# Keys turned once for two units: a turned block of the first batch kept in device memory

## The chip, the cores and the metric

The kernel runs on one core of a Trainium2 chip. Its engines are TensorE (PE, with its weight loads PEld), VectorE (DVE), ScalarE (ACT), GpSimd (POOL) and SyncE (SP), which here issues all the DMAs. Each engine works through its own instructions in the order of the program; semaphores hold an instruction until what it needs is there. The metric is the device time of one execution in microseconds. Before the change it is 1012.05 us, the median of three runs (1011.5 to 1013.39).

## The reference

Three layers one after another: a causal attention with decay, and two feed-forward layers, all in float32.

```python
scores = (1/sqrt(D)) * q @ k.T                      # B=4, H=8, S=576, D=64
cum    = cumsum(log(clip(f, 1e-4, 1)))
scores = where(causal, -1e9, scores + cum_i - cum_j)
x      = softmax(scores) @ v                        # to [2304, 512]
h      = x @ moe_w_in                               # d_ff = 2048
x      = (max(h, 0) + alpha * min(h, 0)) @ moe_w_out
h      = x @ moe2_w_in
g      = where(h >= 1, h, where(h <= -1, 0, (h + 1)**2 / 4))
out    = g @ moe2_w_out
```

The weights come as 64-bit floats; the kernel takes their words apart and builds 32-bit values from them.

## The kernel before

The 576 tokens of a batch are cut into two units: the first has the queries 0 to 255 (QA = 256), the second 256 to 575. A unit is worked in four pairs of heads. For a pair the kernel loads K, Q and V, turns K and Q on PE (a matmul against a unit matrix, 128 tokens at a time, into a PSUM bank), copies them back to SBUF, forms scores, exponentials and the product with V, and writes its part of the first layer's input x. Causality means that a first unit needs the keys 0 to 255, a second one all 576.

The first batch (units 0 and 1) goes through `plain_pair` (line 553), the other three through the code from line 822 on. In `plain_pair`, `load_k` (line 563) and `load_q` (567) load the tokens by `load_tok` (467, two DMAs of whole 128-token blocks and one for a remainder of 64), `ktr` (579) turns K in groups of up to KC = 512 tokens, `kcopy` (585) copies each group to the tile `kT`, and `qk` (646) forms the scores of 64 queries, all of which need every `kcopy` of the pair. `kT` has two buffers, taken in turn by the pairs. A pair of the first unit has one group of 256 tokens: two transposes, one copy. A pair of the second unit has two groups, of 512 and 128 tokens (padded): four transposes and one, a copy of 512 columns and one of 128. The keys 0 to 255 are thus loaded and turned twice, once in each unit. In the later batches the kernel already keeps them: `stash` (line 901) writes the turned block to device memory, `reload` (867) reads it back.

Beside the first batch run the conversion of the first layer's weights (`convert`, 1212: load on line 1227, `mag` 1239, `clamp` 1242, `low_exp` 1248, `top` 1256, `bottom` 1261, `hi` 1269, `lo` 1275) and, as soon as the first 256 tokens of x are there, the first layer's slices (`l1_slice`, 1312; matmuls on lines 1323 and 1362).

The order of each engine's instructions is made by a planner, `Order.emit` (line 114). Every piece of work is a task with an engine, an estimated duration, a position (`pos`), what it depends on and which buffers it takes. The planner plays the program through with these estimates: of the engines it takes the one that can start first, and on it, of the tasks that are ready, the one with the lowest position. DMAs are modelled as one line of transfers (`move`, 182). A task on the made-up engines "X" and "Y" costs no engine's time; "Y" lies 1000 ns ahead of SP. So a task that is added or gone changes the estimated ends of what follows, and with them the orders.

Of the kernel before, what the change touches and what calls it, by code (L numbers as in the profile page):

```python
# [9 lines left out]
F32 = mybir.dt.float32  # L10
# [6 lines left out]
P = 128  # L17
# [176 lines left out]
def kernel(  # L194
# [13 lines left out]
    nc = tc.nc  # L208
# [7 lines left out]
    NKB = -(-S // P)  # L216
    SP = NKB * P
# [4 lines left out]
    QA = 256  # L222
# [3 lines left out]
    RATE = 31  # L226
    SMALL = 0.28
    GLEAD = 4
    JO = 0.5
    QOFF = 0  # L230
    WOFF2 = -5
# [47 lines left out]
    def act(n, bias=False):  # L279
        return 93 + n * 0.833 + (93 if bias else 0)  # L280

    def moved(rows, size):
        return rows * (7.5 + size / 24) / 16

    def tok_issue(t0, t1):
        return (980 if t1 - t0 >= P else 0) + (700 if (t1 - t0) % P else 0)
# [8 lines left out]
    def add(eng, dur, fn, pos, *a, **k):  # L295
        return order.add(eng, dur, fn, pos + PRI.get(fn.__name__, 0), *a, **k)
# [7 lines left out]
    ap1 = la.enter_context(tc.tile_pool(name="ap1", bufs=1))  # L304
# [16 lines left out]
    def x2_at(t0, n):  # L321
# [4 lines left out]
    kept, keep_st = {}, {}  # L326
# [16 lines left out]
        out=count, data0=ident, data1=ident, initial=0.0, op0=ALU.add, op1=ALU.bypass)  # L343
# [47 lines left out]
    KC = 4 * P  # L391
# [42 lines left out]
    for j in range(2):  # L434
        nc.gpsimd.affine_select(
            out=PP[j * D:(j + 1) * D, :D], in_=PP[j * D:(j + 1) * D, :D], pattern=[[-1, D]], compare_op=ALU.is_ge,
# [30 lines left out]
    def load_tok(dst, src, b, pr, t0, t1):  # L467
        n = (t1 - t0) // P
        for j in range(2):
            if n:  # L470
                nc.sync.dma_start(
                    out=dst[:, 0:n, j, :],
                    in_=src[b, 2 * pr + j, t0:t0 + n * P, :].rearrange("(c p) d -> p c d", p=P))
        r = t1 - t0 - n * P
        if r:
            nc.sync.dma_start(
                out=dst[:r, n, :, :],
                in_=src[b, 2 * pr:2 * pr + 2, t0 + n * P:t1, :].rearrange("h p d -> p h d"))
# [16 lines left out]
    def f_tr():  # L495
        fb["p"] = ps_a.tile([P, 512], F32, tag=f"s{fP.slot}", name="pst")
        for b_ in range(NKB):
# [6 lines left out]
        out=fb["f"], in0=fb["f"], scalar1=1e-4, scalar2=1.0, op0=ALU.max, op1=ALU.min), -99, [ft], use=[fB])  # L504
    ft = add("ACT", act(S) + 1300, lambda: nc.scalar.activation(out=fb["f"], in_=fb["f"], func=AF.Ln), -99, [ft],
             use=[fB])
# [21 lines left out]
    last = {}  # L528
# [24 lines left out]
    def plain_pair(u, pr, pos_of, prev_pv):  # L553
        b, q0, q1 = units[u]
        n = q1 - q0
        nk = min(S, -(-q1 // P) * P)
        nt, i0 = n // D, q0 // D
        p0 = pos_of(2 * pr)
        v0 = 0 if u else 2 * (pr % 2)
        kb, qb = Buf(R["raw"]), Buf(R["qr1" if pr % 2 else "qr"])  # L560
        kt, qd, st, sw = Buf(R["k"]), Buf(R[f"qd{pr % 2}"]), Buf(R["st"]), Buf(R["sw"])

        def load_k():
            kb.t = RAW[kb.slot]
            load_tok(kb.t, k, b, pr, 0, nk)

        def load_q():
            qb.t = ph["qr"] if pr % 2 else QR[0]
            load_tok(qb.t, q, b, pr, q0, q1)

        lk = last["lk"] = add("SP", tok_issue(0, nk), load_k, p0 - 3, [last.get("lk")], new=[kb], move=moved(2 * nk, 256))
        lq = last["lq"] = add("SP", tok_issue(q0, q1), load_q, p0 - 3, [last.get("lq")], new=[qb], move=moved(2 * n, 256))
        kready = []
        nkp = -(-nk // P) * P
        for t0 in range(0, nkp, KC):
            t1 = min(nkp, t0 + KC)
            pb = Buf(R["s"])

            def ktr(pb=pb, t0=t0, t1=t1):
                pb.t = ps_a.tile([P, 512], F32, tag=f"s{pb.slot}", name="pst")  # L580
                for c in range(t0 // P, t1 // P):
                    nc.tensor.transpose(pb.t[:, c * P - t0:(c + 1) * P - t0],
                                        kb.t[:, c, :, :].rearrange("p j d -> p (j d)"), ident)

            def kcopy(pb=pb, t0=t0, t1=t1):
                if t0 == 0:
                    kt.t = ap1.tile([P, NKB * P], F32, tag=f"k{kt.slot}", name="kT")
                nc.scalar.copy(out=kt.t[:, t0:t1], in_=pb.t[:, :t1 - t0])

            a = last["ktr"] = add("PE", 112 * (t1 - t0) // P, ktr, p0 - 1, [lk, last.get("ktr")], new=[pb], use=[kb])  # L590
            a = add("ACT", act(t1 - t0), kcopy, p0 - 1, [a] + kready, new=[kt] if t0 == 0 else [],
                    use=[pb] if t0 == 0 else [pb, kt])
            kready.append(a)
        pb = Buf(R["s"])
        np_ = -(-n // P)

# [5 lines left out]
        a = last["qtr"] = add("PE", 112 * np_, qtr, p0 - 1, [lq, last.get("qtr")], new=[pb], use=[qb])  # L602
        qready = []
        for j in range(2):
            def qcopy(pb=pb, j=j):
# [6 lines left out]
                              use=[pb, qd] if j else [pb]))  # L612
# [4 lines left out]
        def choose():  # L617
# [6 lines left out]
                 move=moved(2 * nk, 256))  # L624
# [9 lines left out]
        for g in range(-(-nt // 2)):  # L634
# [3 lines left out]
            for t in tiles:  # L638
# [4 lines left out]
                for x, (a0, a1) in enumerate(parts):  # L643
                    sb = Buf(R["s"])

                    def qk(sb=sb, t=t, a0=a0, a1=a1, x=x, n_=len(parts)):
# [6 lines left out]
                        if x == n_ - 1:  # L653
# [3 lines left out]
                    a = last["pqk"] = add("PE", pe4(a1 - a0) + (a1 - a0) / 2.4 + 120, qk, pg,  # L657
                                          kready + qready + crow_ready + [chosen, last.get("pqk")], new=[sb], use=[kt, qd, sw])
# [3 lines left out]
                for x, (sb, a) in enumerate(sbs):  # L662
                    def low(sb=sb, t=t, x=x, w=parts[x][1] - parts[x][0]):
# [4 lines left out]
                                    use=[sb] if st_new else [sb, st]))  # L668
# [133 lines left out]
    for u, pr in head_list():  # L802
        b, q0, q1 = units[u]
# [56 lines left out]
        for j in range(2):  # L860
            def own(j=j, k_of=k_of):
                k_of(j)
# [3 lines left out]
            if again:  # L866
                def reload(j=j, k_of=k_of, kd=kept[b, pr]):
                    nc.sync.dma_start(out=k_of(j).bitcast(F32)[:, :QA], in_=kd[j])
# [28 lines left out]
        if not again and nk == QA:  # L897
            kept[b, pr] = tc.dram_tile([2, P, QA], F32, name=f"kept{b}_{pr}")
            keep_st[b, pr] = []
            for j in range(2):  # L900
                def stash(j=j, k_of=k_of, kd=kept[b, pr]):
                    nc.sync.dma_start(out=kd[j], in_=k_of(j).bitcast(F32)[:, :QA])
# [1119 lines left out]
```

## Time and profile before

| | |
|---|---|
| median of three runs | 1012.05 us |
| profiled execution, its own time | 1014.81 us |
| span of its profile | 1012.9 us |
| PE busy (matmuls) | 995.4 us, 98% |
| PEld busy (weight loads) | 912.3 us, 90% |
| DVE busy | 775.8 us, 77% |
| ACT busy | 651.0 us, 64% |
| POOL busy | 108.7 us, 11% |
| granted clock of PE | 1.00 throughout |
| read and written in device memory | 95.37 MB, 31.51 MB |

Times in the profile are counted from the start of the span. Busy times are sums over the span; matmuls are pipelined and their ends are modelled, so PE shown as busy is not PE at its peak. The first batch and the first layer's conversion take roughly the first 125 us, the other batches' attention with the rest of the first layer go on to about 540 us, and the second layer follows.

### The profile page before, as it was taken

The numbers are of one execution on the slowest core, as the hardware profiler recorded it, in microseconds if no ns is written. First come the engines' busy times: TensorE is split into PE (matmuls) and PEld (weight loads), VectorE is DVE, ScalarE is ACT, GpSimd is POOL, SyncE is SP. The second block draws the span as 40 slices with busy tenths as digits, with TensorE's granted clock in tenths as the row PEclk, the third lists the DMA queues.
The fourth block names the chain that finished last, engine by engine and source line by source line (L and its number), as shares of the span: only waits on it lengthen the run. The fifth ranks groups of instructions, "written<-read, shape, count | busy, mean of one in ns | idle before, by whom it ended". The sixth has DMA issues, their size and how long they took to land.

```text
span 1012.9 us, 19923 instructions
## 1 busy us (share of the span) xinstructions
PE 995.4 (98%) x6736; PEld 912.3 (90%) x6736; DVE 775.8 (77%) x1874; ACT 651.0 (64%) x1675; POOL 108.7 (11%) x222
## 2 busy tenths in 40 slices
PE   7999999999999999999999999999999999999998
PEld 6788899999999999999998888988889998889886
DVE  7999987887778877788738999987868557565552
ACT  6988789888989888988736555544544334332322
POOL 2000033222322222221100000000000000000000
PEclk9999999999999999999999999999999999999999
DMA  8764223231332213421016668486737544454311
GB/s 263 196 216 140 70 79 96 56 75 34 82 100 58 65 48 72 101 54 39 28 32 217 187 181 256 134 290 236 264 115 249 149 127 121 114 177 125 108 49 63
DMA packets 151222, 128.26 MB, mean 127 GB/s; under 512 B 82720, under 2 KB 121648, under 8 KB 151120
## 3 DMA queue, kind: packets, MB, share of 16 engines
q1 hardware_dynamic: 151120, 126.98, 43.0%
q8 instruction: 54, 0.88, 0.4%
q14 instruction: 48, 0.39, 0.1%
HBM read 95.37 MB, written 31.51 MB: 125 GB/s over the span
## 4 chain that ended last, share of the span: by engine, by line
PE 73%; DVE 5%; ACT 4%; issue 2%; DMA 2%; POOL 0%; SPq 0%; ACTq 0%; DVEq 0%; POOLq 0%
PE ps_z L1601 19%; PE ps_h L1857 12%; PE ps_h L1323 10%; PE ps_y L1362 10%; PE ps_h L1616 7%; PE ps_y L1450 4%; PE ps_h L1406 4%; PE ps_s L991 3%; PE ps_o L1105 1%; DVE S L1066 1%; PE ps_o L1111 1%; PE ps_o L1113 1%; DVE PL L1085 1%; PE ps_o L1112 1%; DVE g L1336 1%
## 5 line engine op out<-in xcount | busy, mean ns | idle before, releaser
L1362 PE MATMUL ps_y<-gg,w 128*128 128x256 f32 x1344 | 183.8, 286 | 0.3 <-DVE gg L1345 0.2
L1323 PE MATMUL ps_h<-x,w 128*128 128x256 f32 x1344 | 183.2, 286 | 0.7 <-DVE g L1336 0.6
L1323 PEld LDWEIGHTS ps_h<-x,w 128*128 128x128 f32 x1344 | 169.1, 191 | 1.3 <-DVE g L1336 1.2
L1362 PEld LDWEIGHTS ps_y<-gg,w 128*128 128x128 f32 x1344 | 169.0, 190 | 1.1 <-DVE gg L1345 0.9
L1601 PE MATMUL ps_z<-w,gw 128*128 128x512 f32 x576 | 149.4, 393 | 0.0
L1857 PE MATMUL ps_h<-xc,wc 128*128 128x384 f32 x672 | 136.6, 338 | 0.0
L1857 PEld LDWEIGHTS ps_h<-xc,wc 128*128 128x128 f32 x672 | 121.1, 188 | 10.3
L1601 PEld LDWEIGHTS ps_z<-w,gw 128*128 128x128 f32 x576 | 106.7, 188 | 15.5
L1895 ACT ACTIVATE t<-t,half 128x384 f32<-128x384 f32 x64 | 39.5, 617 | 70.1 <-DVE t L1892 69.7
L1904 ACT CAST gw<-t 128x384 fp32r<-128x384 f32 x64 | 32.7, 512 | 78.8 <-PE ps_z L1601 75.9
L1005 ACT ACTIVATE S<-ps_s,nb 128x320 f32<-128x320 f32 (+4 forms) x168 | 74.3, 448 | 5.1 <-DVE PL L1085 3.5
L991 PE MATMUL ps_s<-q,kT 128*128 128x320 f32 (+4 forms) x336 | 72.4, 299 | 1.8 <-DVE kT L892 0.8
L1336 DVE SCALAR_TENSOR_TENSOR g<-g,calpha,ps_h 128x256 f32<-128x256 f32 x112 | 53.2, 476 | 26.7 <-ACT g L1333 25.1
L1601 PE MATMUL ps_z<-w,gg 128*128 128x512 f32 x288 | 72.4, 391 | 0.0
L1907 DVE TENSOR_TENSOR gw<-t,gw 128x384 fp32r<-128x384 f32 x64 | 35.6, 556 | 41.3 <-ACT gw L1904 41.0
L545 POOL TENSOR_SCALAR_AFFINE_SELECT S<-S 128x128 f32<-128x128 f32 (+1 forms) x120 | 41.0, 346 | 229.3 <-ACT S L1005 213.0
L1071 ACT ACTIVATE S<-S 128x320 f32<-128x320 f32 (+2 forms) x144 | 59.5, 423 | 8.8 <-DVE S L1066 8.2
L1345 DVE TENSOR_TENSOR gg<-g,gg 128x256 fp32r<-128x256 f32 x112 | 48.9, 438 | 18.9 <-ACT gg L1342 18.0
L1050 POOL PARTITION_ALL_REDUCE pp<-pp x48 | 56.9, 1185 | 60.1 <-ACT pp L1034 25.5
L1601 PEld LDWEIGHTS ps_z<-w,gg 128*128 128x128 f32 x288 | 53.0, 188 | 9.5
L1066 DVE TENSOR_TENSOR S<-pp,S 128x320 f32<-128x320 f32 (+4 forms) x168 | 57.1, 392 | 4.6 <-POOL pp L1050 3.8
L1333 ACT ACTIVATE g<-ps_h 128x256 f32<-128x256 f32 x112 | 42.5, 381 | 23.5 <-PE ps_h L1323 22.5
(178 smaller groups left out, 1944.7 us busy)
## 6 DMA issues: line engine op xcount, KB each, us to landing
wc<-wc SPq DMA_DIRECT2D x112, 256.0 KB
raw<-in_moe_w_in_dram SPq DMA_DIRECT2D x32, 512.0 KB
raw<-in_moe_w_out_dram SPq DMA_DIRECT2D x32, 512.0 KB
wc<-sh SPq DMA_DIRECT2D x32, 256.0 KB
wc<-w SPq DMA_DIRECT2D x24, 256.0 KB
out_dram<-osb SPq DMA_DIRECT2D x18, 256.0 KB
qr<-in_q_dram SPq DMA_DIRECT2D x64, 64.0 KB
wa<-val SPq DMA_DIRECT2D x16, 256.0 KB
```

The source lines that it names most:

```text
L991: nc.tensor.matmul(out=sb.t[:, :m], lhsT=kt.t[:, kb * P:(kb + 1) * P], rhs=qt.t[:, t * NMAX + qo:t * NMAX + qo + m], start=(t == 0), stop= ...
L1005: nc.scalar.activation(out=Sb.t[:, so:so + m], in_=sb.t[:, :m], func=AF.Identity, bias=bias)
L1050: nc.gpsimd.partition_all_reduce(Mb.t[:, :n], Mx.t[:, :n], P, ReduceOp.max)
L1066: nc.vector.tensor_tensor(out=sl, in0=Mb.t[:, qo:qo + m], in1=sl, op=ALU.subtract)
L1071: nc.scalar.activation(out=Sb.t[:, :gn], in_=Sb.t[:, :gn], func=AF.Exp, scale=-SCALE)
L1323: nc.tensor.matmul(out=hb.t, lhsT=a[:, sl], rhs=b, start=(cc == 0 and t == 0), stop=(cc == NCC - 1 and t == 2))
L1336: nc.vector.scalar_tensor_tensor(out=gb.t, in0=gb.t, scalar=calpha[:, s:s + 1], in1=hb.t, op0=ALU.mult, op1=ALU.add)
L1345: nc.vector.tensor_tensor(out=gg.t[1], in0=gb.t, in1=gg.t[0].bitcast(F32), op=ALU.subtract)
L1362: nc.tensor.matmul(out=Y[c][e // 2][:, e % 2, :], lhsT=a[:, sl], rhs=b, start=(s == 0 and t == 0 and e % 2 == 0), stop=(s == NF - 1 and t ...
L1601: nc.tensor.matmul(out=zb.t, lhsT=a, rhs=b, start=(start and t == 0), stop=(stop and t == 2))
L1616: nc.tensor.matmul(out=hb.t, lhsT=a[:, sl], rhs=b, start=(cc == 0 and t == 0), stop=(cc == NCC - 1 and t == 2))
L1857: nc.tensor.matmul(out=hb.t[:, :m], lhsT=wb.t[:, z, sl], rhs=xb.t[y][:, cc, :], start=(begin and cc == 0 and t == 0), stop=(cc == 1 and t ...
```

## The change

A pair of the first unit now writes the turned keys 0 to 255 (128 partitions by 256 columns, 128 KB) to device memory, as a task on SP with position p0 + STP, STP = 3. The pair of the second unit loads only the tokens 256 to 575, turns them in one group of 384 tokens (three transposes, one copy of 384 columns), and reads the kept block back into the same tile. The tile is taken by a task of its own, `own`, on the engine "Y" once K is loaded; the reload depends on it and on the store.

```diff
+    STP = 3
...
+        k0 = QA if u else 0
+
         def load_k():
             kb.t = RAW[kb.slot]
-            load_tok(kb.t, k, b, pr, 0, nk)
+            load_tok(kb.t[:, k0 // P:], k, b, pr, k0, nk)
...
-        lk = last["lk"] = add("SP", tok_issue(0, nk), load_k, p0 - 3, [last.get("lk")], new=[kb], move=moved(2 * nk, 256))
+        lk = last["lk"] = add("SP", tok_issue(k0, nk), load_k, p0 - 3, [last.get("lk")], new=[kb], move=moved(2 * (nk - k0), 256))
...
-        for t0 in range(0, nkp, KC):
+
+        def own():
+            kt.t = ap1.tile([P, NKB * P], F32, tag=f"k{kt.slot}", name="kT")
+
+        owned = add("Y", 0, own, p0 - 1, [lk], new=[kt])
+        if u:
+            def reload(kd=kept[b, pr]):
+                nc.sync.dma_start(out=kt.t[:, :QA], in_=kd)
+
+            kready.append(add("SP", 450, reload, p0 - 1, [owned, keep_st[b, pr]], use=[kt], move=moved(P, 4 * QA)))
+        for t0 in range(k0, nkp, KC):
...
             def kcopy(pb=pb, t0=t0, t1=t1):
-                if t0 == 0:
-                    kt.t = ap1.tile([P, NKB * P], F32, tag=f"k{kt.slot}", name="kT")
                 nc.scalar.copy(out=kt.t[:, t0:t1], in_=pb.t[:, :t1 - t0])
 
-            a = last["ktr"] = add("PE", 112 * (t1 - t0) // P, ktr, p0 - 1, [lk, last.get("ktr")], new=[pb], use=[kb])
-            a = add("ACT", act(t1 - t0), kcopy, p0 - 1, [a] + kready, new=[kt] if t0 == 0 else [],
-                    use=[pb] if t0 == 0 else [pb, kt])
-            kready.append(a)
+            a = last["ktr"] = add("PE", 112 * (t1 - t0) // P, ktr, p0 - 1, [lk, owned, last.get("ktr")], new=[pb], use=[kb])
+            kready.append(add("ACT", act(t1 - t0), kcopy, p0 - 1, [a], use=[pb, kt]))
+        if not u:
+            kept[b, pr] = tc.dram_tile([P, QA], F32, name=f"kept{b}_{pr}")
+
+            def stash(kd=kept[b, pr]):
+                nc.sync.dma_start(out=kd, in_=kt.t[:, :QA])
+
+            keep_st[b, pr] = add("SP", 450, stash, p0 + STP, kready, use=[kt], move=moved(P, 4 * QA))
```

## Rows read from the trace of the kernel before

**Rows 1.** Busy us by stretch: length, PE, PEld, DVE, ACT, POOL, clock, DMA share, GB/s.
```profile
0.00:45.00 45.00, 36.41 (x305) 29.72 (x306) 36.69 (x97) 33.75 (x89) 7.87 (x35) 1.00 0.82 237
45.00:120.00 75.00, 75.00 (x782) 65.01 (x780) 74.49 (x174) 61.40 (x150) 3.32 (x14) 1.00 0.46 140
130.00:500.00 370.00, 365.08 (x2929) 358.82 (x2929) 292.55 (x797) 323.18 (x940) 94.34 (x164) 1.00 0.27 66
```

**Rows 2.** The chain that ended last, 100 to 150 us: start us, us, what.
```profile
128.93 0.43 DVE kT L892
...
147.17 0.50 PE ps_s L991 x2
```

**Rows 3.** PE's waits, 27 to 45 us: us in total, times, longest.
```profile
PE pst L720 <- ACT pp L683: 1.6, 2, 0.8
PE ps_o L743 <- ACT S L725: 0.3, 1, 0.3
PE ps_s L649 <- ACT pp L683: 0.2, 1, 0.2
```

**Rows 4.** Line 582: engine, count, duration ns min/median/max, first and last start us.
```profile
L582 PE MATMUL pst<-ident,raw x28: 272/273/444, 4.2 to 89.7; 128*128 128x128 f32 x28
```

**Rows 5.** Timeline, 35 to 40.5 us, PE, ACT and DVE: start us, us, what.
```profile
35.62 0.60 PE L582 MATMUL pst<-ident,raw 128*128 128x128 f32 x4
36.05 0.69 PE L649 MATMUL ps_s<-kT,qd 128*128 128x256 f32 x2
36.75 0.59 ACT L588 COPY kT<-pst 128x512 f32<-128x512 f32 x1
37.23 0.67 ACT L1269 CAST w<-raw 128x512 fp32r<-128x512 f32 x1
37.67 0.33 PE L582 MATMUL pst<-ident,raw 128*128 128x128 f32 x1
37.84 0.49 PE L600 MATMUL pst<-ident,qr 128*128 128x128 f32 x3
37.93 0.69 DVE L1275 TENSOR_TENSOR w<-raw,w 128x512 fp32r<-128x512 f32 x1 [0.57 <-ACT w L1269]
39.08 0.28 ACT L588 COPY kT<-pst 128x128 f32<-128x128 f32 x1
39.64 0.70 PE L649 MATMUL ps_s<-kT,qd 128*128 128x320 f32 x2
```

**Rows 6.** Groups by line and shape, 0 to 70 us: busy us, mean ns, idle before.
```profile
L588 ACT COPY kT<-pst 128x512 f32<-128x512 f32 x3 | 1.8, 587 | 0.0
L588 ACT COPY kT<-pst 128x256 f32<-128x256 f32 x4 | 1.5, 363 | 0.0
```

**Rows 7.** Lines 902 and 868, the later batches' stores and reloads on SP.
```profile
L902 SPq DMA_DIRECT2D kept<-kT x24: 333/344/448, 118.8 to 405.0; - x24
L868 SPq DMA_DIRECT2D kT<-kept x24: 321/364/585, 162.4 to 466.8; - x24
```

**Rows 8.** Timeline of SP and of ACT: a weight load, and its first read.
```profile
31.75 0.60 SPq L1227 DMA_DIRECT2D raw<-in_moe_w_in_dram  x1
46.90 0.69 ACT L1239 ACTIVATE val<-raw 128x512 f32<-128x512 f32 x1
```

**Rows 9.** Landing of loads: timeline at the start, the chain at 206 us.
```profile
2.16 0.98 SPq L471 DMA_DIRECT2D qr<-in_q_dram  x2
5.27 0.66 PE L600 MATMUL pst<-ident,qr 128*128 128x128 f32 x2 [0.46 <-DMA qr<-in_q_dram]
205.90 2.37 DMA pp<-spread
```

**Rows 10.** Timeline: use of the buffers of the turned K.
```profile
24.86 0.37 ACT L588 COPY kT<-pst 128x256 f32<-128x256 f32 x1
30.57 0.19 PE L654 MATMUL ps_s<-above,identR 128*128 128x64 f32 x1
57.12 0.70 PE L649 MATMUL ps_s<-kT,qd 128*128 128x320 f32 x2
```

## The prediction, made before the result was known

> **What bounds the kernel now.** I read the stages first (busy time of each engine by stretch), then the chain that ended last, then PE's waits, then the instructions of the one stretch that the change touches.
>
> [rows 1] show two kinds of stage. From 130 to 500 us PE is full (365.08 of 370 us, its weight loads 358.82) and DVE has room (292.55): there PE sets the time. From 45 to 120 us, where the first batch's second unit runs beside the conversion of the first layer's weights, PE is shown busy 75.00 of 75 us, but DVE is busy 74.49 of 75 as well, and PE's weight loads only 65.01. The first 45 us are loose for all: PE 36.41, DVE 36.69, ACT 33.75.
>
> The chain says which of the two full engines counts. In [rows 2] it runs through DVE (with ACT between) at 128.93 us and passes to PE at 147.17 us. So up to 147 us what ended last was DVE's row of work, not PE's row of matmuls. Everything that the change touches lies before 92 us.
>
> PE's waits between 27 and 45 us [rows 3] are all on ACT, 1.6, 0.3 and 0.2 us, 2.1 in all. From 130 to 500 us PE idles 4.9 us (370 less 365.08), in many small waits.
>
> **The change, part by part.** *Transposes removed.* There are 28 K transposes on L582 [rows 4]: 8 in the first unit, 20 in the second (four and one for each of four pairs). The change leaves three for each pair of the second unit, so 8 go, and two groups become one. In [rows 5] the four start at 35.62 and the next matmul at 36.05 (0.43 us for four, 0.11 each), the single one at 37.67 and the next at 37.84 (0.17). Four and one cost 0.60; three cost 0.33, with the start of a group some 0.37: about 0.23 us less for each pair, 0.9 us for four. If PE were the bound all the way, 0.9 us would be the gain; the other bound is nothing, where PE only runs sooner into a wait for DVE.
>
> *ACT copies removed.* A pair of the second unit had a copy of 512 columns (587 ns, [rows 6]) and one of 128 (0.28 us at 39.08, [rows 5]); it gets one of 384. Between 363 ns for 256 columns and 587 for 512 that is some 475 ns, so 0.39 us a pair and 1.6 us in all by durations. After 45 us ACT is not full (61.40 of 75 us), so only the first pair's copies count: the copy at 36.75 stands right ahead of the cast at 37.23, for which DVE idles 0.57 us before 37.93 [rows 5]. A copy of 384 columns is over 0.11 us sooner (587 less 475), and DVE with it. DVE is full from 45 to 120 us, so 0.11 us is what the chain up to 147 us gains for sure.
>
> *Loads.* In the second unit two K loads of 128 KB become two of 64 KB; the remainder load of 32 KB stays, so SP issues as many K loads as before. Added are four stores and four reloads of 128 KB each. SP has such instructions later, at 344 and 364 ns [rows 7], so eight cost SP 2.8 us, and what stands behind them is late by up to that much. Mostly these are weight loads, which are ready well ahead: the eleventh is issued at 31.75 us and its piece first read at 46.90 [rows 8], 15 us later. If that cover were gone, DVE would start pieces late and the 2.8 us would be lost in full. In bytes the change adds 0.5 MB (four times 256 KB less 128 KB), which at the 237 GB/s of the first stage is 2.2 us of transfer; the DMA engines are busy 0.82 of those 45 us [rows 1], 8 us free, so I cost it at nothing, and at 2.2 us at most.
>
> *The store's wait, and the buffer.* A turned K may be overwritten only when its store has read it. The first pair's scores begin before 10 us, and the third pair, which takes its buffer, writes at 24.86 [rows 10]: over 14 us, against 0.34 to issue the store and 2 to 3 us to land (below). Nothing waits for it. On SP the store waits for ACT's copy, and behind it stand Q and weight loads; SP's order is worked out with estimates of the same ends, so I take 0, and at most 0.5 us for each store.
>
> *The reload's wait.* It is new on the path: the scores of a pair need it. For the first pair its buffer comes free when the last scores of the first unit's third pair end, at 30.57 + 0.19 = 30.76 us [rows 10]; the scores that need it start at 39.64 [rows 5]. Landing: a Q load issued from 2.16 to 3.14 us held PE until 5.27, 2.1 us after, and a read back from device memory later took 2.37 [rows 9]. Issued at once, the reload is there at 30.76 + 0.36 + 2.37 = 33.5 us, 6 us early. I take 0; the bound above is the slow rival. The second pair has more room: its buffer is the one of the first unit's last pair, and its scores start at 57.12 [rows 10].
>
> *Sum.* On the profiled execution, 1014.81 us (span 1012.9 and 1.91 around it): ACT's 0.11, and the first pair's transposes, 0.23, which lie ahead of 45 us where PE still waits; the other three pairs' 0.7 us I take at nothing, by the chain. That is -0.34, so about 1014.4. The median of the runs shown is 1012.05, 2.76 below the profiled one; -0.4 from it gives 1011.6.
>
> The Trainium skill (Perfetto Trace Analysis, Identifying the Most-Contended Engine) says that the busy share of matmuls is no good measure of TensorE's headroom and that of weight loads is a better one. The trace agrees, in [rows 1]: PE's matmuls are full in both stages, while weight loads fall from 358.82 of 370 us to 65.01 of 75. By this rule the removed transposes of that stretch are worth nothing and the sum is -0.1 to -0.3; by the matmul row it would be -0.9.
>
> **The rivals.** *Slower: the reload of the first pair comes late.* It is one transfer with one price. From 31.75 us SP issues weight pieces of 512 KB between the K and Q loads, and at 237 GB/s such a piece takes 2.2 us. With the reload issued at 36 us, behind two pieces, it lands at 36 + 2.4 + 4.4 = 42.8 us; it decides from 39.64 on, so PE would wait some 3.2 us there, and DVE, whose reductions read those scores, with it. For it: 0.82 of the DMA engines' time is taken up. Against it: 6 us of room, and the planner ranks the reload ahead of the weights. 1012.05 + 3.2 - 0.3 = 1015.0.
>
> The Trainium skill (DMA: Bandwidth & Descriptors, Queues, rings and completion order) says that a DMA engine takes up the descriptors of one ring in the order of the ring, so that a reload would stand behind the weights. No row here shows a reload in that stretch; by this rule it comes out as in this rival, if two pieces are ahead.
>
> *Faster: the loose stage tightens.* PE's 2.1 us of waits between 27 and 45 us go, because the shorter copies and the scores of the first pair, tied to one copy instead of the late one at 39.08, let PE and DVE through; with the 0.9 us of transposes 1012.05 - 3.0 = 1009.0. For it: ACT is the engine waited for. Against it: most of what PE waits for there is the exponential of the first unit's last pair, which the change does not shorten.
>
> *It gives nothing at all*, since DVE holds PE to 147 us: 1012.0, inside the forecast.
>
> *The order of later work is drawn anew* in each of these cases, since the planner gets other ends for all that follows. The 4.9 us of PE's idle time between 130 and 500 us can grow or shrink by a part of it, say 1.5 us; that widens every case and has no sign.
>
> **How the numbers follow.** A measurement of this kernel tells 0.2%, about 2 us, from no change. Forecast, with the case of no gain at all, 1011.6 and its own range 1010.2 to 1013.2: chance 0.52, no change. Faster rival: 0.27. Slow rival, or a bad draw of the order beyond 2 us: 0.21. The range reaches into both rivals: 1008.8 to 1014.6.
>
> **What would show it.** Right: 20 K transposes and eight copies to the turned K, DVE busy to 99% from 45 to 120 us as before, PE's 0.9 us found again as waits between 110 and 147 us, and the scores of the first pair starting within 1 us of 39.6. Wrong: DVE idle between 45 and 120 us; PE waiting for the reloaded K; an idle time of PE from 130 to 500 us that is more than 2 us off 4.9, in which case the order and not the stage decides.

## The result, and the profile after

The changed kernel takes 1019.98 us, the median of five runs (1019.58 to 1020.55), against 1011.86 of the kernel before in five runs beside it (1011.5 to 1013.39): a ratio of 1.0071, 95% interval 1.0056 to 1.0085. It is slower by 8.1 us. The ratios here and below are estimates from all the executions on both sides, not quotients of the two medians (here 1.0080). Forecast were 1011.6 and a range up to 1014.6, so the time lies outside the range. The profiled execution took 1019.74 us, its span is 1018.0.

The stages first, as in [rows 1], with two stretches added that will matter (columns: stretch, length, busy us and instructions of PE, PEld, DVE, ACT and POOL, granted clock, DMA share, GB/s). The kernel after:

```profile
0.00:45.00 45.00, 36.83 (x305) 29.76 (x306) 37.57 (x98) 34.67 (x92) 8.03 (x35) 1.00 0.76 220
45.00:120.00 75.00, 75.00 (x786) 65.67 (x785) 74.17 (x174) 59.50 (x145) 3.86 (x17) 1.00 0.51 158
0.00:130.00 130.00, 121.76 (x1195) 104.78 (x1196) 119.61 (x290) 100.51 (x253) 13.01 (x57) 1.00 0.59 178
130.00:500.00 370.00, 361.39 (x2876) 353.95 (x2875) 290.13 (x783) 322.04 (x935) 94.32 (x164) 1.00 0.27 67
120.00:200.00 80.00, 76.49 (x635) 73.46 (x634) 63.85 (x172) 67.85 (x203) 21.41 (x38) 1.00 0.33 85
280.00:340.00 60.00, 57.23 (x443) 55.90 (x442) 48.42 (x131) 53.37 (x153) 14.06 (x26) 0.97 0.30 76
```

The same view of the kernel before, of the stretches that [rows 1] does not have:

```profile
0.00:130.00 130.00, 121.06 (x1190) 103.89 (x1191) 119.84 (x290) 102.19 (x259) 14.36 (x59) 1.00 0.59 175
120.00:200.00 80.00, 78.23 (x658) 76.14 (x658) 65.85 (x174) 69.51 (x209) 22.75 (x42) 1.00 0.33 85
280.00:340.00 60.00, 59.20 (x478) 58.51 (x477) 48.90 (x133) 53.62 (x152) 15.46 (x27) 1.00 0.31 75
```

The stretch that the change touches is as good as before: DVE is busy 74.17 of 75 us, and by 130 us PE has done 1195 matmuls against 1190, with eight fewer to do. Counted by the work of the kernel before (eight removed transposes added) that is 1203, so PE is 13 matmuls ahead. Then it falls behind: from 130 to 500 us it does 2876 against 2929, 53 fewer, in two places, 23 fewer from 120 to 200 us and 35 fewer from 280 to 340; elsewhere it makes up a few. The records of both traces are complete (6736 matmuls before, 6728 after), so the counts can be used. A matmul there takes 370 / 2929 = 0.126 us on average; 53 are 6.7 us, less the 13 it was ahead (1.6 us) 5.1 us, and the spans differ by 5.1. The rest up to 8.1 lies in the executions: the profiled one of before was 2.95 us over its median, that of after 0.24 under its own. Why is taken up below the table.

Idle time alone would not have told this. It grew from 4.92 to 8.61 us in these 370 us, by 3.7. The other 3 us lie in time in which PE is shown busy and does fewer matmuls, in part because its clock fell (0.97 on average from 280 to 340 us); the count sees them, the busy column does not.

What the prediction said of the changed pairs, in the rows that answer to [rows 4] and [rows 6], the K transposes and the copies to the turned K (columns as there):

```profile
L595 PE MATMUL pst<-ident,raw x20: 272/273/448, 3.9 to 82.4; 128*128 128x128 f32 x20
```

```profile
L599 ACT COPY kT<-pst 128x384 f32<-128x384 f32 x4 | 1.9, 470 | 0.0
...
L599 ACT COPY kT<-pst 128x256 f32<-128x256 f32 x4 | 1.5, 363 | 0.0
```

Twenty and eight, the copy of 384 columns at 470 ns (taken: 475). The first reload on SP, and the first scores that need it on PE, which answer to [rows 5]:

```profile
33.32 0.59 SPq L585 DMA_DIRECT2D kT<-kept  x1
```

```profile
37.97 0.81 PE L665 MATMUL ps_s<-kT,qd 128*128 128x320 f32 x2
```

The scores start 1.7 us sooner than before (39.64), with no wait for the reload. The wait on SP itself was longer than thought, for the later pairs:

```profile
L585 SPq DMA_DIRECT2D kT<-kept x4: 338/433/594, 33.3 to 78.5; - x4
L585 SPq EVENT_SEMAPHORE  x3: 17/1852/12339, 38.7 to 66.1; - x3
```

The last reload held SP for 12.3 us, from 66.1 to 78.4, and all loads behind it. The cover was there: DVE is busy 10.00 of the 10 us from 70 to 80.

The chain of the kernel after, 100 to 150 us (answers to [rows 2]; start us, us, what). It passes between DVE, PE and ACT, and at 149 us it is still on DVE, where that of before had passed to PE:

```profile
128.41 1.49 PE ps_h L1339 x12
...
149.08 0.49 DVE g L1352
```

The largest of PE's waits of the kernel after, 130 to 500 us (us in total, times, longest):

```profile
PE ps_h L1339 <- DVE g L1352: 3.5, 3, 2.4
```

Before, this was 0.6 us in one wait. The longest one, 2.4 us, lies at 290 us, 200 us behind the last thing that the change touches. The timeline around it, ACT, DVE and PE (start us, us, what, in brackets the idle time before it and what ended it):

```profile
288.47 0.42 ACT L948 CAST q<-pst 64x320 fp32r<-64x320 f32 x1
...
288.90 0.42 ACT L941 CAST q<-pst 64x320 fp32r<-64x320 f32 x1
...
289.34 0.42 ACT L948 CAST q<-pst 64x320 fp32r<-64x320 f32 x1
289.66 0.41 ACT L1087 ACTIVATE S<-S 128x256 f32<-128x256 f32 x1
...
290.10 0.38 ACT L1349 ACTIVATE g<-ps_h 128x256 f32<-128x256 f32 x1
...
290.32 0.62 DVE L1082 TENSOR_TENSOR S<-pp,S 128x256 f32<-128x256 f32 x2
...
290.86 0.42 DVE L1101 TENSOR_TENSOR PL<-S,PH 128x256 fp32r<-128x256 f32 x1
...
291.31 0.48 DVE L1352 SCALAR_TENSOR_TENSOR g<-g,calpha,ps_h 128x256 f32<-128x256 f32 x1
...
291.85 1.97 PE L1339 MATMUL ps_h<-x,w 128*128 128x256 f32 x12 [2.39 <-DVE g L1352]
```

It is read from the bottom. PE needs a PSUM bank for the next slice; it is free when DVE (L1352) has combined the slice before; that needs ACT's L1349, which stands in ACT's order behind three casts of q and an exponential; and from 290.48 us, when L1349 has ended, L1352 stands for 0.83 us more in DVE's own order behind L1082 and L1101. PE waited for none of these. I read this as an unlucky order and not as an engine that is too slow; experiment 5 tests it.

### The profile page after: what moved, and what is told of

Same layout as the page of the kernel before. It is cut to its first block, busy times and chain, and to the rows that moved or that the text cites. A ratio compares the mean times of both kernels' runs of the same rounds, so it can differ in the third digit from the quotient of the medians.

```text
span 1018.0 us, 19903 instructions
## 1 busy us (share of the span) xinstructions
PE 997.4 (98%) x6728; PEld 913.3 (90%) x6728; DVE 777.9 (76%) x1874; ACT 650.5 (64%) x1671; POOL 109.0 (11%) x222
## 4 chain that ended last, share of the span: by engine, by line
PE 77%; DVE 10%; ACT 6%; issue 3%; DMA 2%; SPq 1%; POOL 0%; ACTq 0%; DVEq 0%; POOLq 0%
PE ps_z L1617 19%; PE ps_h L1873 12%; PE ps_y L1378 10%; PE ps_h L1339 10%; PE ps_h L1632 7%; PE ps_y L1466 4%; PE ps_h L1422 4%; PE ps_s L1007 3%; PE ps_s L665 1%; PE ps_o L1121 1%; PE ps_o L1129 1%; DVE S L1082 1%; PE ps_o L1127 1%; ACT S L1021 1%; DVE g L1352 1%
## 5 line engine op out<-in xcount | busy, mean ns | idle before, releaser
L1617 PEld LDWEIGHTS ps_z<-w,gw 128*128 128x128 f32 x576 | 106.7, 188 | 15.5
L1352 DVE SCALAR_TENSOR_TENSOR g<-g,calpha,ps_h 128x256 f32<-128x256 f32 x112 | 53.5, 478 | 29.4 <-ACT g L1349 27.9
L1082 DVE TENSOR_TENSOR S<-pp,S 128x320 f32<-128x320 f32 (+4 forms) x168 | 57.7, 394 | 4.8 <-POOL pp L1066 4.3
L1358 ACT CAST gg<-g 128x256 fp32r<-128x256 f32 x112 | 45.4, 405 | 19.5 <-DVE g L1352 18.7
```

What stands on the lines that cost most here:

```text
L1082: nc.vector.tensor_tensor(out=sl, in0=Mb.t[:, qo:qo + m], in1=sl, op=ALU.subtract)
L1352: nc.vector.scalar_tensor_tensor(out=gb.t, in0=gb.t, scalar=calpha[:, s:s + 1], in1=hb.t, op0=ALU.mult, op1=ALU.add)
L1617: nc.tensor.matmul(out=zb.t, lhsT=a, rhs=b, start=(start and t == 0), stop=(stop and t == 2))
```

## The experiments

The theory from here on: the change's work costs next to nothing, and the 8 us are the order of the later batches, which the planner draws anew because the first batch ends at other times. The rival: the work itself (the DMAs, the waits on SP) costs them. The planner's order can be taken apart from the work: an order is a list of tasks, with the buffers that each takes, which a kernel can play instead of planning. In experiments 1 to 5 and 9 to 11 the edit is such a list, made from the lists of the two planners:

```diff
+def emit_written_out(self):
...
+    while p < len(raw):
+        i, n = struct.unpack_from("<HB", raw, p)
+        t = self.tasks[i]
...
+        t.fn()
+
+
+Order.emit = emit_written_out
+SEQ = (
...
```

**1. The change's work, the order of before.** The eight added DMAs stand where the changed kernel has them among SP's tasks.

> The changed kernel's work in the order of the kernel before: every engine's order is written out, each task stands where it stood before, the four stores and four reloads are put behind the SP instruction that they follow in the changed kernel. Theory 1, the re-drawn order is the loss: 1011 to 1013 us, no change. Theory 2, the work itself is (stores, reloads and their waits in the first batch): about 1020 us. Both at once would lie between, near 1016.

Measured: 1013.33 us against 1013.1, ratio 1.000 (0.999 to 1.001). The stretch of this kernel's profile:

```profile
130.00:500.00 370.00, 365.48 (x2935) 359.44 (x2934) 292.33 (x797) 323.67 (x941) 93.51 (x163) 1.00 0.26 66
```

With the old order PE does 2935 matmuls there, and idles 4.5 us. The whole change, with its stores, reloads and waits, costs at most some 2 us (1013.33 is just above the forecast 1011 to 1013), so as the cause of the 8 us the rival falls. That it costs exactly nothing is not shown: the 23 executions of before beside this kernel lie in two groups, ten up to 1011.93 and thirteen from 1012.92, and their median is at the lower edge of the upper one; beside the later experiments it was 1011.1 to 1011.9.

**2. The work of before, the order of after.** The list is the changed kernel's, less the eight DMAs, with the second group of turned K put behind the first.

> The work of the kernel before (no store, no reload, all of K loaded and turned in the second unit) in the order of the changed kernel; the second group's transpose and copy stand right behind the first group's. Theory 1 (order): 1018 to 1021 us. Theory 2 (work): 1011 to 1013 us.

Measured: 1022.61 against 1013.1, 1.0092 (1.0077 to 1.0107), without a single instruction of the change.

```profile
130.00:500.00 370.00, 360.65 (x2879) 352.80 (x2879) 289.73 (x784) 321.00 (x932) 93.54 (x163) 1.00 0.27 67
```

The same loss in the same stretch, 2879 matmuls. The order does it alone; the time is 1.6 us above the forecast 1018 to 1021.

**3 and 4. The two orders joined at about 120 us.** In the first the change's work in its own order up to 120 us, then in that of before; in the second the work of before in its own order, then in that of after.

> The changed kernel in its own order for what its planner starts in the first 120 us (all of the first batch), and in the order of the kernel before for the rest. Theory 1 as I hold it, that the loss is in the later batches (the wait of 2.39 us at 289 us and the clock that falls after it): 1010 to 1013 us. If the first batch's own order or its reloads are the loss: 1018 to 1021 us.

> The unchanged work, in its own order up to 120 us of the planner's time and in the changed kernel's order after that: nothing of the change is in it but the later order. Theory 1, later batches: 1017 to 1021 us, with PE's wait of over 2 us near 289 us and a lower granted clock behind it. Otherwise 1011 to 1013 us.

Measured: 1015.22, ratio 1.0028 (1.0017 to 1.0039), and 1022.25, ratio 1.0084 (1.0068 to 1.01), both against 1013.1 and both above their forecasts (1010 to 1013 and 1017 to 1021). The loss goes with the order behind 120 us. The 0.28% of the first kernel are not the first batch's alone: where its two orders are joined, from 125 to 130 us, PE is busy 3.44 of 5 us (4.93 in the changed kernel). What the first batch does is taken up below.

**5. One slice moved.** The order of after, with the Relu and the combination of the one slice that held PE at 290 us put ahead.

```diff
 ACT
+  Relu of the slice (L1349)
   cast of q (L948), cast of q (L941), cast of q (L948), exponential (L1087)
-  Relu of the slice (L1349)
```

> The changed kernel in its own order, but for one slice of the first layer: its Relu on ACT stands three casts and an exponential earlier, its combination on DVE one cast, two subtractions and one more earlier (two instructions moved, nothing else). PE's wait of 2.39 us at 289 us is for exactly this DVE instruction. If that wait is a cost of its own: 2 to 4 us faster than the changed kernel (2 for the wait, up to 1.7 more if the granted clock no longer falls behind it), so some 8 us slower than before becomes 4 to 6: 1017 to 1019 us where before stands at 1013. If the wait only gathers what was late anyway, no gain: 8 us slower than before.

Measured: 1018.54 against 1011.9, 1.0059 (1.0042 to 1.0077), an interval that overlaps that of the changed kernel's 1.0071; but all six executions (1017.97 to 1019.22) lie below all five of the changed kernel. The wait is gone to 0.40 us, and others stand behind it (timeline of PE, this kernel):

```profile
288.94 1.69 PE L1339 MATMUL ps_h<-x,w 128*128 128x256 f32 x12 [0.40 <-DVE g L1352]
...
291.21 0.38 PE L1127 MATMUL ps_o<-PH,vH 128*128 128x256 f32 x1 [0.57 <-ACT vH L964]
```

PE does its 6728 matmuls in the same order in both kernels, so the same matmul can be looked up in both. Ahead of the moved slice this kernel is 0.93 us ahead, behind it 1.98 (the changed kernel first):

```profile
315.93 0.42 PE L1127 MATMUL ps_o<-PH,vH 128*128 128x320 f32 x1 [0.17 <-ACT pp L1160]
```

```profile
313.95 0.42 PE L1127 MATMUL ps_o<-PH,vH 128*128 128x320 f32 x1 [0.17 <-ACT pp L1160]
```

So a wait of 2.39 us was worth 1.05 us at its place, not the 2 to 4 forecast, and by 480 us the lead is down to 1.41: some 0.4 us are left of it, three more matmuls from 130 to 500 us. The other 0.9 us were there before 130 us, in the same order, most of them by a clock that rose to full at 20.68 us instead of 23.44 (taken up below the table). So my reading of the longest wait as the place to mend was wrong: PE came 2 us sooner to its next matmuls and waited there, for a cast of V first. Most of the loss belongs to the sequence of many tasks, not to the one that the list of waits puts on top.

**6 and 12. No change but an estimate.** The work of before, with the planner's estimate of the first batch's K copies 10 ns lower, and in another kernel 40 ns higher. Not an operation differs, only the orders.

```diff
-            a = add("ACT", act(t1 - t0), kcopy, p0 - 1, [a] + kready, new=[kt] if t0 == 0 else [],
+            a = add("ACT", act(t1 - t0) - 10, kcopy, p0 - 1, [a] + kready, new=[kt] if t0 == 0 else [],
```

> The kernel before, with the same work: only the planner's estimate of the copy of the turned K (first batch, 12 tasks) is 10 ns shorter, so the planner draws another order. If any re-drawing can cost what the change cost, this lies outside 2 us of the kernel before, slower by 2 to 9 us. If the order of the kernel before is nothing special and only the changed kernel's is bad: within 2 us.

> The kernel before with nothing changed but the planner's estimate of the first batch's K copies, 40 ns higher; the work is the same, the orders of the engines differ in some 160 to 300 places. Theory (the order drawn anew costs by itself, whatever the work): a ratio that is not 1.000, by the draws so far between 1.001 and 1.008, 1012.5 to 1020 us. Rival (only orders drawn with the change's work lose): 1.000, 1011 to 1012.5 us.

Measured: 1013.28 against 1011.9, 1.0012 (1.0 to 1.0025); and 1015.82 against 1011.12, 1.0033 (1.002 to 1.0046). An order drawn anew with no change behind it costs up to 0.3%; the first of the two stays within the 2 us that were forecast for no effect, and its interval reaches 1.0, so it alone would not show a cost. These draws are also smaller ones than the changed kernel's. From some 200 us on, the orders of PE, ACT and DVE are those of the kernel before again, instruction for instruction, while the changed kernel's differ until some 480 us; from 280 to 340 us, where the changed kernel lost most, PE is busy 59.19 and 59.18 of 60 us in these two, as before.

**7 and 8. The change, with another draw.** The changed kernel, with the estimate of its K transposes 40 ns higher, or that of its K copies.

```diff
-            kready.append(add("ACT", act(t1 - t0), kcopy, p0 - 1, [a], use=[pb, kt]))
+            kready.append(add("ACT", act(t1 - t0) + 40, kcopy, p0 - 1, [a], use=[pb, kt]))
```

> The changed kernel with all its work; only the planner's estimate of a group of K transposes (first batch) is 40 ns longer, so another order is drawn. If the loss is a bad draw and nothing of the work: 2 us either side of the kernel before, well below the changed kernel. If the change's work costs: still 1018 or more where before stands at 1013.

> As the last one, another draw: the estimate of the copy of the turned K is 40 ns longer. The same two forecasts; the spread between this and the last one tells how much one draw differs from the next, which I expect to be 1 to 5 us.

Measured: 1014.49 and 1013.96 against 1011.9, 1.0021 (1.0008 to 1.0034) and 1.0014 (1.0003 to 1.0025). The same work as in the changed kernel, 5 to 6 us faster than it, though a little over the 2 us that were forecast. So 5 to 6 of its 8 us are that one draw. These two orders, too, are again that of before, from some 200 and 250 us on, and PE is busy 59.2 of 60 us from 280 to 340.

**9 and 10. The orders joined at about 240 us**, to part the two places: the work of before with the order of after from there on, and the changed kernel with the order of before from there on.

> The work of the kernel before, without the change. Its own order up to about 240 us, and from there the order of the changed kernel. In the earlier run with the new order from 120 us on, time was lost in two places, between 120 and 200 us and around 290 us; this kernel has only the second. Theory (two places, each with a loss of its own): PE loses 3 to 5 us more than before between 280 and 340 us and nothing ahead of it, 1015 to 1017 us, ratio 1.003 to 1.005; the wait of the second feed-forward's first matmul for DVE's g, 2.4 us at 290 us, is seen again. Rival (one loss, that between 120 and 200 us, which later work only carries on): no loss from 240 us on, 1011 to 1013 us, ratio 1.000. Rival (the order as a whole): 1019 to 1021 us.

> The changed kernel with its own order up to about 240 us, and from there the order of the kernel before: the counterpart of the run beside it. Theory (two places): only the loss between 120 and 200 us is left, 1014 to 1017 us, ratio 1.003 to 1.005, and no wait over 1 us between 280 and 340 us. Rival (one loss, ahead of 240 us): 1019 to 1021 us. Rival (the place around 290 us is all): 1011 to 1013 us. The two runs' losses over the kernel before should add up to the 8 us of the change, within 1.5 us.

Measured: 1016.14 against 1011.12, 1.0047 (1.0032 to 1.0061), and 1017.2, 1.0056 (1.0043 to 1.0069), the second just above its forecast of 1.003 to 1.005. The two stretches, the first kernel and then the second:

```profile
120.00:200.00 80.00, 78.06 (x642) 75.94 (x642) 65.26 (x175) 70.22 (x211) 24.48 (x45) 1.00 0.31 79
...
280.00:340.00 60.00, 57.16 (x452) 55.87 (x452) 49.15 (x132) 53.02 (x151) 14.73 (x25) 1.00 0.29 72
```

```profile
120.00:200.00 80.00, 76.58 (x637) 73.61 (x635) 63.98 (x171) 67.84 (x203) 21.32 (x38) 1.00 0.34 86
...
280.00:340.00 60.00, 59.22 (x477) 58.39 (x476) 48.34 (x135) 54.08 (x157) 14.89 (x26) 1.00 0.30 75
```

Each has one of the two idle times of the changed kernel (57.23 and 76.49) and not the other. They are two separate losses, each made where its order is, as the theory had it. In times they do not add up: the two ratios make 1.03%, 0.3% more than the changed kernel lost; I had said within 1.5 us. Part of that is in the second kernel, ahead of 130 us:

```profile
49.05 1.65 PE L759 MATMUL ps_o<-vF,S 128*64 128x64 f32 x24 [1.72 <-DMA vF<-in_v_dram]
```

Another part is the joint of the two orders. From 250 to 260 us PE waits 0.94 us in the second kernel and does 66 matmuls, in the changed kernel 79 (columns as above, the second kernel first):

```profile
250.00:260.00 10.00, 8.84 (x66) 8.05 (x64) 7.53 (x19) 7.50 (x24) 2.90 (x6) 1.00 0.16 47
```

```profile
250.00:260.00 10.00, 9.78 (x79) 9.40 (x77) 8.18 (x22) 8.97 (x27) 3.51 (x6) 1.00 0.25 71
```

On the same matmul it falls back there from 0.19 us behind the changed kernel to 1.95. So a joined kernel has a loss of its own, and that the matmuls from 130 to 500 us seem to add up, 21 and 29 fewer than before against 53 of both, is in part luck. The profiled execution of the first of the two was the fastest of its six, 1.7 us under their median.

**11. One added store later.** The kernel of experiment 1, in which PE waited 1.22 us at 20.74 us for a load of Q that stood behind the second pair's store on SP; the store is put behind the loads of Q and K.

```diff
 SP
-  store of the turned keys, second pair
   load of weights, load of Q, load of K
+  store of the turned keys, second pair
   load of V
```

> The change's work in the order of the kernel before, as in the first experiment, but with the second pair's store moved behind the loads of Q and K of the fourth pair of the first unit. In the first experiment the store stood ahead of a weight load and these loads, SP held for a landing of an earlier DMA behind it, and the Q load began at 20.22 us (18.74 before); PE waited 1.2 us for it. Theory (each added DMA on SP holds up what is behind it until an earlier one has landed): the Q load begins near 18.7 us, PE's wait for it is below 0.3 us, and the time is 0 to 1.2 us below the first experiment's, so 1011 to 1012.5, ratio 0.999 to 1.000. Rival (DVE sets the time up to 147 us, so PE's wait there costs nothing): ratio 1.000 as in the first experiment, with the wait gone.

Measured: 1013.03 against 1011.12, 1.0012 (1.0002 to 1.0022), above the forecast of 0.999 to 1.000. The Q load begins at 18.53 us instead of 20.22, the wait is gone, and no time came of it (the time of the first experiment stands against other runs of before, so only the ratios are set side by side: 1.000 and 1.0012). The rival, that a wait of PE there costs nothing, fits; it is not proved, since this kernel was profiled in an execution in which the clock rose late (below) and PE came later to that place anyway. No version beats the kernel before.

**All the kernels in one measure.** PE's matmuls by 130 us and from there to 500 us, from the same view of each profile. Where a kernel has the change's work, the eight transposes that it need not do are added to the first number.

| kernel | by 130 us | 130 to 500 us | span, us | ratio of times |
|---|---|---|---|---|
| before | 1190 | 2929 | 1012.9 | 1 |
| after | 1203 | 2876 | 1018.0 | 1.0071 |
| 1 change, old order | 1206 | 2935 | 1010.6 | 1.000 |
| 11 the same, a store later | 1195 | 2928 | 1012.5 | 1.0012 |
| 2 old work, new order | 1184 | 2879 | 1020.3 | 1.0092 |
| 3 new order to 120 us | 1202 | 2919 | 1012.7 | 1.0028 |
| 4 new order from 120 us | 1192 | 2868 | 1020.7 | 1.0084 |
| 5 one slice moved | 1212 | 2879 | 1016.6 | 1.0059 |
| 9 new order from 240 us | 1220 | 2908 | 1012.7 | 1.0047 |
| 10 new order to 240 us | 1200 | 2900 | 1015.3 | 1.0056 |
| 6 estimate -10 ns | 1219 | 2917 | 1011.1 | 1.0012 |
| 12 estimate +40 ns | 1218 | 2913 | 1011.4 | 1.0033 |
| 7 change, other draw | 1206 | 2913 | 1014.1 | 1.0021 |
| 8 change, other draw | 1217 | 2923 | 1011.1 | 1.0014 |

The sum of the two columns gives the span: 0.126 us for each matmul above or below the 4119 of before, from 1012.9, meets the other thirteen within 1.2 us. Kernels wholly in the old order do 2928 to 2935 in the second stretch, the draws of experiments 6, 7, 8 and 12 2913 to 2923, and those with all of the changed kernel's later order 2868 to 2879.

The first column varies with something else. Two executions of the same work in the same order (up to 247 us), the kernels before and of experiment 9, at the same two matmuls on PE:

```profile
20.43 1.20 PE L649 MATMUL ps_s<-kT,qd 128*128 128x256 f32 x2
```

```profile
18.00 0.68 PE L649 MATMUL ps_s<-kT,qd 128*128 128x256 f32 x2
```

In the first PE still ran at the lower speed at 20 us, in the second at the higher one at 18 us. The trace's own records of the granted clock say the same: the first record of full clock begins at 24.05 us in the kernel before and at 15.29 in experiment 9. The clock column of the views counts time without a record as full, so its 1.00 does not show this, in the table ahead of the prediction either. PE's lead is 3.65 us at 24 us, and all of it is there at 240. In matmuls by 130 us it is 1220 instead of 1190. Of the fourteen profiles, those of experiments 1, 3, 6, 8, 9, 10 and 12 have the early rise (13.3 to 15.5 us), the others a late one (20.7 to 24.1). This fits the 2.95 us by which the profiled execution of before lies over its median; of the other executions no trace was kept, so that most of them rose early is argued, not shown.

The changed kernel's order makes less of an early rise. Experiments 3 and 10 have its order and work up to 120 us and beyond. The same matmuls of the changed kernel (rise at 23.44 us), of experiment 3 (13.51) and of experiment 10 (15.47):

```profile
119.78 1.68 PE L1378 MATMUL ps_y<-gg,w 128*128 128x256 f32 x12
```

```profile
118.03 1.68 PE L1378 MATMUL ps_y<-gg,w 128*128 128x256 f32 x12
```

```profile
120.15 1.68 PE L1378 MATMUL ps_y<-gg,w 128*128 128x256 f32 x12
```

Experiment 3 was 3.23 us ahead of the changed kernel at 48 us and is 1.75 ahead here; experiment 10 was 2.77 ahead and is 0.37 behind. Both lost it at about 49 us, where PE, sooner at its work, waited 1.52 and 1.72 us for a load of V; in experiment 10 the clock fell behind the wait as well (last section). Part of this is the change's work and not its order: SP issues that load at 45.05 us in experiment 10, at 44.12 in experiment 1, with the old order, and at 41.59 in experiment 9, which has the old order without the added DMAs and whose PE did not wait for V.

```profile
45.05 1.19 SPq L472 DMA_DIRECT2D vF<-in_v_dram  x2
```

```profile
41.59 1.65 SPq L471 DMA_DIRECT2D vF<-in_v_dram  x2
```

So the change's work has a price that the ratio of experiment 1 hides. DVE does its instructions in one and the same order in the kernel before and in experiments 1 and 11. On the same instruction, experiment 11 (late rise) stays 0.4 to 0.6 us ahead of before from 16 to 200 us: the work costs nothing. Experiment 1 (early rise) goes from 0.2 us ahead of experiment 9 at 20 us to 1.7 behind from 80 us on: it costs 1.9 us.

The 8.1 us between the medians are thus 6.7 of the later order, less 1.6 by which the changed kernel was ahead at 130 us, and some 3 that an early rise gives to the kernel before and, for the most part, not to the changed one. The last term rests on one trace of each kernel, as said.

## Why the prediction was wrong

*What failed* is the step "the order of later work is drawn anew". It was named, with its place (PE's idle time between 130 and 500 us) and its sign of being wrong (over 2 us off 4.9), and that sign came true at 8.61. Its size was the error: taken at 1.5 us, measured at 6.7 us, and between 0.8 and 6.7 us over the five draws (2923 to 2876 matmuls, by 0.126 us). The four small ones are those whose order met the old one again by some 200 or 250 us; this one ran on to 480. I took a part of the idle time as the measure of what an order can do. But the growth of the idle time is only some half of what this order costs, 3.7 of 6.7 us, and the idle time before sets no bound for it. "Has no sign" was wrong too: all five draws, with the change's work or without, came out slower, by 0.12 to 0.71% (the smallest with an interval that reaches none).

*The slow rival* held a late reload, and "a bad draw of the order beyond 2 us" beside it. The draw was it. The reload was issued at 33.32 us, and its scores began at 37.97 without a wait. Where the clock rose early and PE came sooner, in experiment 8, it was late by 0.41 us (timeline of PE), far from the 3.2 of the rival:

```profile
34.92 0.78 PE L665 MATMUL ps_s<-kT,qd 128*128 128x320 f32 x2 [0.41 <-DMA kT<-kept]
```

In neither kernel was a load of weights issued on SP in the five us ahead of the reload, so a reload behind two such loads was not put to the test. What the Trainium skill (DMA: Bandwidth & Descriptors, Queues, rings and completion order) says, that descriptors are consumed in the order of their ring, is borne out or denied by no run here.

*The terms of the sum.* -0.34 us, by ACT's shorter copy and the transposes: experiment 1 measured 0 within 0.1%, which neither shows nor denies a third of a microsecond (the sum then took it as -0.4). In the same order with a late rise, experiment 11 against before, DVE's lead grows from 0.41 us at 20 us to 0.61 at 130, so 0.2 of the 0.34 us are seen there. The faster rival's first half came true and bought nothing: the scores came 1.7 us sooner, outside the 1 us around 39.6 that was named as a sign of being right, and PE was 13 matmuls ahead at 130 us. The eight DMAs "at nothing": so it was where the clock rose late, in the changed kernel even with SP held for 12.3 us. Where it rose early PE waited up to 1.7 us at a time for loads of Q, K or V (experiments 1, 3, 8 and 10; up to 0.75 with the work of before in 6, 9 and 12), and the work cost 1.9 us in experiment 1.

*DVE holds the stage from 45 to 120 us:* right, busy to 99% again. The 0.9 us of transposes were to be found again as waits of PE before 147 us. PE's idle time from 120 to 200 us did grow, by 1.7 us, but experiments 2 and 4 show the same growth with the transposes in place; so it is the order's, and the step was not confirmed.

## What to carry to other kernels

Where a planner writes the order, any change is two changes: time it once in the old order, written out, and judge the work by that; judge the draw by nudging an estimate where nothing else changes (here +0.12 and +0.33%), and look how far the new order runs before it meets the old one again. A kernel joined from two orders has a loss at the joint. Count the matmuls done in a stretch rather than the idle time; the count accounts for the span. Where two kernels have the same order, look up the same instruction in both: the difference of its starts tells what a wait has cost by then, which need not be the wait's length. A term "the order is drawn anew" belongs in the range with the size that such draws have shown, here up to 0.7%, not as a share of the idle time.

## What the runs showed of the hardware that was not expected

The granted clock does not rise at the same time in each execution: matmuls of one shape took 1.20 us at 20 us in one execution and 0.68 us at 18 us in another of the same early work, worth 3.65 us in the order of before and at most 1.75 in the changed kernel's (above).

It also fell again in the middle of some executions, from the level of 2.4 to that of 1.2 GHz, behind a wait of PE. Stretches of 2 us (columns as above), of the kernel after behind its wait of 2.39 us and of experiment 10 behind the one of 1.72 us:

```profile
294.00:296.00 2.00, 2.00 (x11) 2.00 (x10) 1.94 (x6) 1.78 (x6) 0.00 (x0) 0.50 0.59 133
```

```profile
50.00:52.00 2.00, 2.00 (x19) 1.88 (x16) 1.11 (x3) 0.22 (x1) 0.00 (x0) 0.50 0.94 324
```

In 294 to 296 us PE did 11 matmuls, where 18 is usual in that neighbourhood. A wait does not always bring it. Experiments 2 and 4 have the same later order and nearly the same wait in it, 2.37 and 2.39 us; in experiment 2 the clock stayed at 1.00, in experiment 4 it fell as in the changed kernel (0.97 on average from 280 to 340 us in both). At this wait experiment 4 is 0.65 us ahead, and 24 us later, on the same matmul, 0.42 behind (experiment 2 first):

```profile
316.94 0.42 PE L1111 MATMUL ps_o<-PH,vH 128*128 128x320 f32 x1 [0.18 <-ACT pp L1144]
```

```profile
317.36 0.42 PE L1111 MATMUL ps_o<-PH,vH 128*128 128x320 f32 x1 [0.17 <-ACT pp L1144]
```

So the fall cost 1.1 us there. In experiment 5, where the clock did not fall either, the gain of 1.05 us holds both the shorter wait and the clock; the two were not parted.
